# Linear attention into a Swish layer on one core: the first two batches' kv in quadrants, the numerators in rows of 64, and a new order of the start

## The chip, the core and the metric

The kernel runs on one core of a Trainium2 chip. A core has a matrix engine (PE, whose weight loads the profile lists as PEld), a vector engine (DVE), an activation engine (ACT), a general engine (POOL) and a queue engine (SP). The engines run on their own and wait for each other by semaphores; each takes its instructions in order. Results of PE land in PSUM, eight banks of 512 f32 values on each of 128 partitions; everything else lives in SBUF, and DMA queues move data to and from memory. The metric is the device time of one execution in microseconds (us). Before the change three runs took 277.32, 277.26 and 275.57 us, a median of 277.26.

## The reference

Inputs are q, k and v of 8 batches, 8 heads, 576 positions and 64 elements, and the weights `w_in` (512 x 2048), `w_out` (2048 x 512) and `beta` (2048).

```python
phi = lambda x: np.where(x > 0, x, np.exp(x) - 1.0) + 1.0
q_p, k_p = phi(q), phi(k)
kv  = einsum('bhsd,bhse->bhde', k_p, v)      # 64 x 64 for each head
z   = sum(k_p, axis=2)
num = einsum('bhsd,bhde->bhse', q_p, kv)
den = einsum('bhsd,bhd->bhs', q_p, z)[..., None] + 1e-6
x   = (num / den)                            # rows (b, s), columns (h, d): 4608 x 512
h   = x @ w_in
g   = h * sigmoid(beta * h)
out = g @ w_out                              # 4608 x 512, f32
```

## The kernel before

**Layout.** A batch's 576 positions are 64 groups of 9 (`G`, `J`). Heads are held in fours: `pr` (0 or 1) picks a block of four heads, a row half `a` of the 128 partitions and an index `il` within the half pick the head. `phi` is the minimum of an exponential on ACT (`phi_exp`, L162) and `max(x, 0) + 1` on DVE (`phi_relu`, L167; `phi_min`, L174). A batch's positions make four tiles of 128 rows (t = 0 to 3), which H and Y of the batch use, and a tile of 64 rows (t = 4), which goes to `xT_tail` and is worked off for all batches together at the end.

**A batch.** phi(k) and v give kv (and z, as a 65th column of ones in `vaug`, from batch 1 on). phi(q) is transposed, the numerators are a product of its transpose and kv, DVE divides by the denominators into `xs_sb`, and the result is transposed again into `xT`. H is 16 blocks `ff` of 128 columns, four matmuls each over 512 columns (`h_mm`, L401), followed by Silu on ACT (`silu`, L409), which writes `g`. Y of batch 0 is 16 quarters `y_mm(0, t, i)`: tile t, and four blocks of `w_out_sb[i]`, four matmuls each (L416). From batch 1 on, Y uses a scheme with fewer products (`y_fast`, L796).

**Order.** The program's order is written out by hand (`manual_schedule`): each engine takes its instructions in the order of the text, and only the semaphores are made by the framework. A PSUM tile gets one of the slots of its pool and has to wait until the last reader of the slot's tile before it is done; accesses of two engines to one bank of one tile are put in the order of the text. Before the change there are four single banks for the whole run (`bank`, pool `hps`), four more for the start (`bank1`, pool `fps`), and after `first.close()` (L630) two pairs of banks (`banks`, pool `wps`) in place of the latter.

**The start, batch 0 (L482 to L629).** q and k are loaded in halves on the SP queue, v in two halves (`v0b`) on the POOL queue, held back by a small copy `gate` that needs the first half of q. `idle(n)` issues n matmuls of 512 columns whose result nobody reads. After phi(q) and its transposes (`q_half`, `q_last`), DVE copies the first half of the transposes (`q_copy`, L505) ahead of `phi_min` of k's first half, and ACT copies the second (L544). PE then sums phi(k) over the positions (`z_sums`, L515) and forms kv with 128 columns for a pair of heads at once (`kv_first`, L526), of which half is not wanted: DVE masks it (`kv_mask`, L535). `zbd` (L553) spreads z to a masked matrix, twenty matmuls give the denominators `dps` (L563), `denom` (L570, L571) adds 1e-6 and inverts them, `numer_first` (L582, L586) gives the numerators in four matmuls over all 128 rows and divides, `x_first` transposes and copies, and `h_first(t)` does four blocks of H for 128 columns of tile t. The order on PE is z_sums(0), kv_first(0), z_sums(1), the denominators, kv_first(1), numerators of three tiles, and then transposes, H and the rest of the numerators by turns. Twelve blocks of H over 512 columns follow.

**Between H of batch 0 and H of batch 1 (L640 to L711).** Here `w_out` is scaled by 1/beta (`w_out_scale`, L450 and L452), phi of batch 1 is made, and Y of batch 0 is interleaved with kv of batch 1 (`kv_both`, L222), which is copied in two casts of 64 partitions into a block matrix `kv_bd` (L234), its numerators (`numer_mm`, L297; `numer_xs`, L308 to L310), their transposes (`x_trans`, L381) and phi of batch 2. From batch 2 on kv goes to `kv_q` with one cast (L230).

Of the kernel before, what the change touches and what calls it, by code (L numbers as in the profile page):

```python
# [16 lines left out]
def kernel(  # L17
# [29 lines left out]
    first = ExitStack()  # L47
    fps = first.enter_context(tc.tile_pool(name="fps", bufs=4, space=bass.MemoryType.PSUM))
# [4 lines left out]

    def bank1(name, shape=None, dt=F32):
        return fps.tile(shape or [P, 512], dt, tag="f", name=name)
# [62 lines left out]
    kv_bd = consts.tile([P, 2, 2, 2, EA], BF16)  # L118
    nc.gpsimd.memset(kv_bd, 0.0)
# [19 lines left out]
    kvmask = consts.tile([P, 2, 2, EA], BF16)  # L139
    nc.vector.memset(kvmask, 0.0)  # L140
    nc.vector.memset(kvmask[:D, :, 0, :], 1.0)
    nc.vector.memset(kvmask[D:P, :, 1, :], 1.0)
# [4 lines left out]

    warm_ps = bank("warm_ps")
# [24 lines left out]
    def phi_min(b, a, pr):  # L173
        nc.vector.tensor_tensor(  # L174
            st[b, a][:, pr].rearrange("p j (h d) -> p j h d", h=2),
            st[b, a, pr, "e"].rearrange("p h j d -> p j h d"),
            st[b, a, pr, "r"].rearrange("p h j d -> p j h d"),
            ALU.min,
        )
# [32 lines left out]
    def kv_both(b):  # L212

        t = banks("kvp")
        for pr in range(2):
            for j in range(J):
                for il in range(2):  # L220
                    for a in range(2):
                        nc.tensor.matmul(  # L222
                            t[half(il), a, pr * EA : (pr + 1) * EA],
                            st[b, "k"][half(a), pr, j, il * D : (il + 1) * D],
                            vaug[b % 2][half(a), pr, j, il, 0:EA],
                            start=(j == 0), stop=(j == J - 1), skip_group_check=True,
                        )
        tv = t[:, :, 0 : 2 * EA].rearrange("p a (r e) -> p a r e", r=2)
        if b > 1:
            nc.vector.tensor_copy(kv_q[b % 2], tv)  # L230
            return
        st[b, "kv"] = kv_bd.rearrange("p a r h e -> p a r (h e)")
        for il in range(2):
            nc.vector.tensor_copy(kv_bd[half(il), :, :, il], tv[half(il)])  # L234
# [42 lines left out]
    def q_stat(b, t, hh, pr, n):  # L277
        if (b, "qTd") in st:
            return st[b, "qTd"][:, hh, pr * J + 2 * t : pr * J + 2 * t + n // G, :].rearrange(
                "p j g -> p (j g)"  # L280
            )
        return st[b, "qT"][:, pr, t, hh, 0:n]

    def rows_of(t):
        return P if t < NT - 1 else G

    def xs_tile(b, t):
        st[b, "xs", t] = xs_sb.rearrange("p i n -> p (i n)")[:, t * DM : (t + 1) * DM]
        n = rows_of(t)
        return st[b, "xs", t][:n].rearrange("p (i a d) -> p a i d", a=2, d=D)  # L290

    def numer_mm(b, t):
        n = rows_of(t)
        nps = st[b, "nps", t] = banks("nps")
        for hh in range(2):
            for pr in range(2):
                nc.tensor.matmul(  # L297
                    nps[:n, hh, pr * 2 * EA : (pr + 1) * 2 * EA],
                    q_stat(b, t, hh, pr, n), st[b, "kv"][:, hh, pr, :],
                    start=True, stop=True, skip_group_check=True,  # L300
                )

    def numer_xs(b, t):
        n = rows_of(t)
        nv = st[b, "nps", t][:n, :, 0 : 4 * EA].rearrange("p a (h e) -> p a h e", h=4)
        den = work.tile([P, 2, 7], F32, tag="den", name="den")[:, :, 0:4]
        rden = work.tile([P, 2, 7], F32, tag="rden", name="rden")[:, :, 0:4]
        nc.vector.tensor_scalar(den[:n], nv[:, :, :, D], 1e-6, None, ALU.add)  # L308
        nc.vector.reciprocal(rden[:n], den[:n])
        nc.vector.tensor_mul(  # L310
            xs_tile(b, t), nv[:, :, :, 0:D], rden[:n, :, :, None].to_broadcast([n, 2, 4, D])
        )
# [58 lines left out]
    def x_dst(b, t):  # L371
        if t < NT - 1:
            return xT[b % 2][:, :, 2 * t : 2 * t + 2].rearrange("p i r n -> p r i n")
        return xT_tail[:, :, b].rearrange("p i r n -> p r i n")

    def x_trans(b, t, eng, tp=None):
        n = rows_of(t)
        if tp is None:
            tp = banks("xtp", [P, KC, P], BF16)
        for p in range(KC):  # L380
            nc.tensor.matmul(  # L381
                tp[:, p, :n], st[b, "xs", t][:n, p * P : (p + 1) * P], identity[:n, :n],
                is_transpose=True, start=True, stop=True, skip_group_check=True,
            )
        copy(eng, x_dst(b, t), tp[:, :, :n].rearrange("p (r i) n -> p r i n", i=2))

    def x_trans_dma(b, t=NT - 1):
        for pr in range(2):
            nc.sync.dma_start_transpose(
                out=xT_tail[:, :, b, pr],  # L390
                in_=st[b, "xs", t][: rows_of(t), pr * HM : (pr + 1) * HM],
            )
# [98 lines left out]
    qtp = [bank1("qtp", [P, 1024], BF16) for _ in range(2)]  # L491
    phi_part(0, "q", 0)
    q_half(0, 0, qtp[0])
    idle(3)
    phi_part(0, "q", 1)
    q_half(0, 1, qtp[1])
    t8 = bank1("qtp8", [P, 2 * P], BF16)
    q_last(0, t8)
    bps = bank("bps", [P, FC])
    nc.tensor.matmul(bps, beta_row, ident16, is_transpose=True, start=True, stop=True)  # L500
    idle(4)
    x = xin(0, "k", 0)
    phi_exp(0, "k", 0, x)
    phi_relu(0, "k", 0, x)
    q_copy(nc.vector, 0, 0, qtp[0])  # L505
    phi_min(0, "k", 0)


    zps = [bank("zps") for _ in range(2)]
# [10 lines left out]
    kvp0 = [bank1("kvp0") for _ in range(2)]  # L520
    kv0 = consts.tile([P, 2, 2, 2 * D], BF16)

    def kv_first(pr):
        for j in range(J):
            for hh in range(2):
                nc.tensor.matmul(  # L526
                    kvp0[hh][:, pr * P : (pr + 1) * P],
                    st[0, "k"][half(hh), pr, j, :],
                    v0b[half(hh), 2 * pr : 2 * pr + 2, j, :],
                    start=(j == 0), stop=(j == J - 1), skip_group_check=True,  # L530
                )

    def kv_mask(pr):
        for hh in range(2):
            nc.vector.tensor_mul(  # L535
                kv0[:, hh, pr].rearrange("p (h d) -> p h d", h=2),
                kvp0[hh][:, pr * P : (pr + 1) * P].rearrange("p (h d) -> p h d", h=2),
                kvmask[:, hh, :, 0:D],
            )

    z_sums(0)
    idle(1)
    phi_part(0, "k", 1)
    q_copy(nc.scalar, 0, 1, qtp[1])  # L544
# [3 lines left out]
    kv_first(0)  # L548
    z_sums(1)
    idle(1)  # L550
    kv_mask(0)
    for hh in range(2):
        nc.vector.tensor_mul(  # L553
            zbd[:, hh], zps[hh][:, 0:2, None].to_broadcast([P, 2, 2]), kvmask[:, :, :, 0]
        )
    dps = bank("dps", [P, NT, 2, 2, 2])
    den0 = consts.tile([P, NT, 8], F32)
    rden0 = consts.tile([P, NT, 8], F32)
    for t in range(NT):
        n = rows_of(t)  # L560
        for hh in range(2):
            for pr in range(2):
                nc.tensor.matmul(  # L563
                    dps[:n, t, hh, pr], st[0, "qT"][:, pr, t, hh, 0:n], zbd[:, hh, pr, :],
                    start=True, stop=True, skip_group_check=True,
                )
    dv = dps.rearrange("p t a b c -> p t (a b c)")
# [5 lines left out]
    kv_first(1)  # L573
    denom(P, slice(0, NT - 1))
    kv_mask(1)

    def numer_first(t):
        n = rows_of(t)
        nps = bank1("nps0", [P, 2, 2, P])
        for hh in range(2):  # L580
            for pr in range(2):
                nc.tensor.matmul(  # L582
                    nps[:n, hh, pr], st[0, "qT"][:, pr, t, hh, 0:n], kv0[:, hh, pr, :],
                    start=True, stop=True, skip_group_check=True,
                )
        nc.vector.tensor_mul(  # L586
            xs_tile(0, t),
            nps[:n].rearrange("p a b (c d) -> p a (b c) d", d=D),
            rden0[:n, t].rearrange("p (a i) -> p a i", a=2)[:, :, :, None].to_broadcast(
# [3 lines left out]

    def x_first(t, eng):
        x_trans(0, t, eng, bank1("xtp0", [P, KC, P], BF16))

# [3 lines left out]
    def h_first(t):  # L600
        if not hp0:
            hp0.extend(bank("h_ps") for _ in range(4))
        for ff in range(4):
            h_mm(xT[0], ff, hp0[ff], t * P, (t + 1) * P)

    for t in range(3):
        numer_first(t)
    denom(G, slice(NT - 1, NT))
    x_first(0, nc.scalar)
    numer_first(3)  # L610
    x_first(1, nc.scalar)
    h_first(0)
    numer_first(4)
    x_first(2, nc.scalar)
    h_first(1)
    x_first(3, nc.scalar)
# [3 lines left out]
    nc.vector.reciprocal(rbeta, beta_c)  # L620
    h_first(2)
    x_first(4, nc.vector)
    h_first(3)
    for ff in range(4):
        silu(0, ff, hp0[ff])
    for ff in range(4, 8):
        hp = bank1("h_ps")
        h_mm(xT[0], ff, hp)
        silu(0, ff, hp)  # L629
    first.close()  # L630
    wps = ctx.enter_context(tc.tile_pool(name="wps", bufs=2, space=bass.MemoryType.PSUM))
# [20 lines left out]
    phi_min(1, "q", 0)  # L652
    phi_min(1, "q", 1)
# [18 lines left out]
    w_out_scale(nc.scalar, 3)  # L672
    for t in range(2):
        y_mm(0, t, 2, yps[t])
    kv_both(1)
    phi_tile(2, "q")
    phi_tile(2, "k")
    y_mm(0, 2, 2, yps[2])
    numer(1, 0)
    y_mm(0, 3, 2, yps[3])  # L680
# [247 lines left out]
```

## Time and profile before

| | |
|---|---|
| profiled execution, device time | 276.86 us |
| its span, first to last instruction | 275.1 us |
| median of three runs | 277.26 us |
| PE busy | 267.2 us, 97% of the span |
| DVE, ACT, POOL busy | 168.2, 173.4, 44.3 us |
| granted TensorE clock, mean | 0.991 |
| PE busy from 0 to 17.80 us | 14.48 us |
| PE busy from 17.80 to 42.68 us | 24.78 of 24.88 us |
| PE busy from 42.68 to 51.92 us | 8.65 of 9.24 us |
| PE busy from 51.92 us on | 219.35 of 223.18 us |

Times in the views are counted from the first instruction. The timeline gives start and length in us, engine, line, operation and tile, the number of instructions merged into the row, and in brackets the idle time of the engine before it with what ended it. The chain of waits follows the execution back from its last instruction, at each step to what released it. A busy PE is not a PE at full speed: the column PEclk says what share of its clock was granted.

### The profile page before, as it was taken

Reading aid. Unit: us, or ns where it says so; the run is one execution under the profiler, and the core shown is the slowest. Engines: PE = TensorE matmul, PEld = TensorE weight load, DVE = VectorE, ACT = ScalarE, POOL = GpSimd, SP = SyncE. Lnnn points to the kernel's source line nnn. Section 1 sums busy time; section 2 is a strip of 40 time slices with the busy share of each in tenths; the row PEclk is TensorE's granted clock in tenths of the full one; section 3 lists DMA queues with packets and bytes.
Section 4 is the critical chain, followed back from the end, with each engine's and each line's share of the span. In section 5 each row is a group of like instructions: output and inputs, shape, how many; then the busy total and the mean of one; then the engine's idle time right before and its main releaser. Section 6 shows DMA issues by size and latency. Waiting matters only on the chain.

```text
span 275.1 us, 6478 instructions
## 1 busy us (share of the span) xinstructions
PE 267.2 (97%) x2756; PEld 173.2 (63%) x2761; DVE 168.2 (61%) x322; ACT 173.4 (63%) x237; POOL 44.3 (16%) x64
## 2 busy tenths in 40 slices
PE   7799999999999999999999999999999999999994
PEld 2585455445865487548754875488548845874693
DVE  4771775999896687566757685768463513342532
ACT  5728897976875785579457946794573077117600
POOL 5822102034003122131213112300000000000000
PEclk9979999999999999999999999999999999999998
DMA  7999999467978996996599659965530040032013
GB/s 255 237 206 351 262 382 256 150 110 225 219 112 170 287 176 115 283 212 65 103 281 211 78 99 279 223 75 88 153 75 13 21 133 0 2 71 82 2 38 114
DMA packets 48956, 42.76 MB, mean 155 GB/s; under 512 B 30352, under 2 KB 40736, under 8 KB 48928
## 3 DMA queue, kind: packets, MB, share of 16 engines
q0 software_dynamic: 13040, 23.40, 36.6%
q1 hardware_dynamic: 35568, 18.75, 32.1%
q8 instruction: 21, 0.34, 0.5%
q10 hardware_dynamic: 320, 0.20, 0.2%
q14 instruction: 7, 0.06, 0.1%
HBM read 36.71 MB, written 9.44 MB: 168 GB/s over the span
## 4 chain that ended last, share of the span: by engine, by line
PE 92%; DVE 3%; DMA 2%; issue 1%; SPq 0%; ACT 0%; DVEq 0%
PE h_ps L401 46%; PE yd L796 10%; PE ya L796 10%; PE yb L796 9%; PE yc L796 5%; PE y_ps L416 4%; DMA stage<-in_k_dram 2%; PE kvp L222 2%; PE nps L332 2%; PE yb L768 1%; PE xtp L381 1%; DVE r L167 1%; PE nps L582 1%; DVE phi_k L174 1%; PE nps L297 1%
## 5 line engine op out<-in xcount | busy, mean ns | idle before, releaser
L409 ACT ACTIVATE g<-h_ps,beta_c 128x512 bf16<-128x512 f32 x144 | 97.6, 687 | 62.0 <-PE h_ps L401 61.8
L401 PE MATMUL h_ps<-xT,w_in 128*128 128x512 bf16 (+1 forms) x560 | 114.5, 361 | 0.1
L401 PEld LDWEIGHTS <-w_in 128*128 128x128 bf16 x624 | 57.4, 98 | 62.1 <-issue 0.2
L796 PEld LDWEIGHTS <-stage 128*128 128x128 bf16 x480 | 46.9, 98 | 5.6 <-issue 0.2
L796 PEld LDWEIGHTS <-g 128*128 128x128 bf16 x384 | 37.5, 98 | 6.0
L796 PE MATMUL ya<-w_out,g 128*128 128x256 bf16 x256 | 30.6, 273 | 0.0
L723 DVE TENSOR_TENSOR stage<-g 128x1024 bf16<-128x1024 bf16 x16 | 12.6, 787 | 22.0 <-ACT g L409 22.0
L727 DVE TENSOR_TENSOR stage<-g 128x1024 bf16<-128x1024 bf16 x16 | 11.8, 739 | 21.8 <-ACT g L409 21.8
L240 POOL CAST vaug<-vf 128x1152 bf16<-128x1152 f32 x11 | 13.6, 1259 | 40.5 <-DMA vf<-in_v_dram 40.5
L347 DVE TENSOR_TENSOR xs_sb<-nps,rden 128x448 bf16<-128x448 f32 (+2 forms) x24 | 18.2, 758 | 0.8
L162 ACT ACTIVATE e<-xk 128x1152 bf16<-128x1152 bf16 (+1 forms) x15 | 16.7, 1160 | 2.2 <-DMA xk<-in_k_dram 2.2
L162 ACT ACTIVATE e<-xq 128x1152 bf16<-128x1152 bf16 x14 | 15.6, 1159 | 1.4 <-DMA xq<-in_q_dram 1.1
L820 DVE TENSOR_TENSOR u<-yc,r 128x512 f32<-128x512 f32 x8 | 5.5, 691 | 17.5 <-PE yc L796 16.6
L155 ACT ACT_TABLE_LOAD x12 | 15.4, 1283 | 0.2
L796 PE MATMUL yd<-ws,stage 128*128 128x256 bf16 x128 | 15.3, 273 | 0.0
L796 PE MATMUL yc<-ws,stage 128*128 128x256 bf16 x128 | 15.3, 273 | 0.0
L796 PE MATMUL yd<-ws,g 128*128 128x256 bf16 x128 | 15.3, 273 | 0.0
L416 PE MATMUL y_ps<-w_out,g 128*128 128x512 bf16 x60 | 14.6, 379 | 0.3 <-issue 0.2
L174 DVE TENSOR_TENSOR phi_q<-e,r 128x1152 bf16<-128x1152 bf16 x16 | 12.3, 766 | 3.7 <-ACT e L162 2.6
L401 PE MATMUL h_ps<-xT_tail,w_in 128*128 128x512 bf16 x64 | 14.0, 379 | 0.0
L367 POOL COPY xT_tail<-xT 128x256 bf16<-128x256 bf16 x6 | 3.1, 518 | 65.4 <-DMA xT<-xs_sb 65.4
L174 DVE TENSOR_TENSOR phi_k<-e,r 128x1152 bf16<-128x1152 bf16 x16 | 12.8, 803 | 1.4
(101 smaller groups left out, 256.5 us busy)
## 6 DMA issues: line engine op xcount, KB each, us to landing
vf<-in_v_dram POOLq DMA_DIRECT2D x7, 1152.0 KB, 9.2
out_dram<-y SPq DMA_DIRECT2D x29, 256.0 KB, 3.8
xq<-in_q_dram POOLq DMA_DIRECT2D x7, 576.0 KB, 12.2
xk<-in_k_dram POOLq DMA_DIRECT2D x7, 576.0 KB, 15.4
w_in<-in_moe_w_in_dram POOLq DMA_DIRECT2D x4, 512.0 KB, 12.7
g<-in_moe_w_out_dram POOLq DMA_DIRECT2D x2, 1024.0 KB, 18.1
stage<-in_moe_w_out_dram POOLq DMA_DIRECT2D x2, 1024.0 KB, 21.3
stage<-in_q_dram SPq DMA_DIRECT2D x2, 576.0 KB, 4.1
```

The costliest lines, as they stand in the source:

```text
L155: nc.scalar.activation(act0, warm[:, 0:1], func)
L162: nc.scalar.activation(e, x, ACTF.Exp)
L174: nc.vector.tensor_tensor(st[b, a][:, pr].rearrange("p j (h d) -> p j h d", h=2), st[b, a, pr, "e"].rearrange("p h j d -> p j h d"), st[b, ...
L222: nc.tensor.matmul(t[half(il), a, pr * EA : (pr + 1) * EA], st[b, "k"][half(a), pr, j, il * D : (il + 1) * D], vaug[b % 2][half(a), pr, j, ...
L240: eng.tensor_copy(dst, src)
L347: nc.vector.tensor_mul(xs_sb[:, ils, v0 * D : v1 * D].rearrange("p i (u d) -> p i u d", d=D), pv[:, :, :, 0:D], rden[:, :, :, None].to_bro ...
L401: nc.tensor.matmul(hp[:, c0:c1].rearrange("p (t n) -> p t n", n=n), w_in_sb[ff // 4][:, kc, (ff % 4) * P : (ff % 4 + 1) * P], xm, start=(k ...
L409: nc.scalar.activation(g_sb[b % 2][:, ff, :], hp, ACTF.Silu, scale=beta_c[:, ff : ff + 1])
L416: nc.tensor.matmul(yp[:, c0:c1], g_sb[b % 2][:, ff, t * P : (t + 1) * P], w_out_sb[i][:, c, c0:c1], start=(ff == 0), stop=(ff == FC - 1), ...
L723: nc.vector.tensor_sub(gs[2][:, c], g[:, c, 0:HM], g[:, c, HM:512])
L727: nc.vector.tensor_add(gs[0][:, c], g[:, c, HM:512], g[:, c2, HM:512])
L796: nc.tensor.matmul(ps[:, p * HM : (p + 1) * HM], lhs(c, p), rhs(c), start=(first and p == 0 and c == 0), stop=True, skip_group_check=True,)
```

## The change

The kv matrices of batches 0 and 1 are formed head by head in quadrants of PE (64 rows by 64 columns), so that nothing has to be masked; `kv_mask`, `kv_bd` and its memset on POOL go. The numerators of both batches are made with 64 rows of contraction, eight matmuls for a tile instead of four, the two row halves into two banks. The column order of `xs_sb` changes with that, and with it the copies into `xT`. PSUM is four single banks and two pairs from the start on. In the single banks sit `zps` (two), `t8b` (the last transposes of q, beta, and the denominators) and `warm_ps`; later one bank `xtp0` for all transposes of the start and three for the first blocks of H, so that `h_first` does three blocks instead of four and a thirteenth follows over 512 columns. On PE, kv_first(0) and half of kv_first(1) come ahead of z_sums(1), the other half ahead of the denominators, and the denominators are made tile 0 first. The first copy of q's transposes moves from DVE to ACT, ahead of phi(k); `phi_min` of k's second half is done in two halves. There are three more `idle` matmuls. In the stretch after H of batch 0, three quarters of Y stand ahead of `kv_both(1)` instead of two, one between it and the numerators, none between the first two numerators; the scaling of `w_out_sb[3]` is shared by ACT and POOL; and `phi_min` of q stands ahead of `phi_relu` of k.

```diff
-        st[b, "kv"] = kv_bd.rearrange("p a r h e -> p a r (h e)")
-        for il in range(2):
-            nc.vector.tensor_copy(kv_bd[half(il), :, :, il], tv[half(il)])
+        nc.vector.tensor_copy(
+            kv_q[b % 2], t[:, :, 0 : 2 * EA].rearrange("p a (r e) -> p a r e", r=2)
+        )
...
     def numer_mm(b, t):
-        n = rows_of(t)
+        n, e = rows_of(t), EA if b else D
         nps = st[b, "nps", t] = banks("nps")
-        for hh in range(2):
-            for pr in range(2):
-                nc.tensor.matmul(
-                    nps[:n, hh, pr * 2 * EA : (pr + 1) * 2 * EA],
-                    q_stat(b, t, hh, pr, n), st[b, "kv"][:, hh, pr, :],
+        for pr in range(2):
+            for a in range(2):
+                for il in range(2):
+                    c = 2 * pr + a
+                    nc.tensor.matmul(
+                        nps[:n, il, c * e : (c + 1) * e],
+                        st[b, "qT"][half(il), pr, t, a, 0:n],
+                        (kv_q[1] if b else kv0)[half(il), a, pr, :],
...
+    zps = [bank("zps") for _ in range(2)]
+    t8b = bank("t8b")
     warm_ps = bank("warm_ps")
...
     phi_part(0, "q", 1)
-    q_half(0, 1, qtp[1])
+    q_copy(nc.scalar, 0, 0, qtp[:, 0])
+    q_half(0, 1, qtp[:, 1])
...
-    q_copy(nc.vector, 0, 0, qtp[0])
-    phi_min(0, "k", 0)
+    phi_part(0, "k", 0)
...
+    kvp0 = banks("kvp0")
+    kv0 = consts.tile([P, 2, 2, D], BF16)
+
+    def kv_first(pr, ils=range(2)):
+        for il in ils:
+            for j in range(J):
+                for a in range(2):
+                    nc.tensor.matmul(
+                        kvp0[half(il), a, pr * D : (pr + 1) * D],
+                        st[0, "k"][half(a), pr, j, il * D : (il + 1) * D],
+                        v0b[half(a), 2 * pr + il, j, :],
...
     z_sums(0)
-    idle(1)
-    phi_part(0, "k", 1)
+    idle(2)
+    x = xin(0, "k", 1)
+    phi_exp(0, "k", 1, x)
+    phi_relu(0, "k", 1, x)
+    for il in range(2):
+        phi_min(0, "k", 1, slice(il, il + 1))
...
     kv_first(0)
+    kv_first(1, (0,))
     z_sums(1)
-    idle(1)
-    kv_mask(0)
+    kv_first(1, (1,))
     for hh in range(2):
         nc.vector.tensor_mul(
-            zbd[:, hh], zps[hh][:, 0:2, None].to_broadcast([P, 2, 2]), kvmask[:, :, :, 0]
+            zbd[:, hh], zps[hh][:, 0:2, None].to_broadcast([P, 2, 2]), ilmask
         )
+    nc.vector.tensor_copy(kv0, kvp0[:, :, 0:P].rearrange("p a (r d) -> p a r d", r=2))
...
+    def x_first(t, eng):
+        if not xtb:
+            xtb.append(bank("xtp0", [P, KC, P], BF16))
+        x_trans(0, t, eng, xtb[0])
...
+    def h_first(t, ffs=range(3)):
+        if not hp0:
+            hp0.extend(bank("h_ps") for _ in range(3))
+        for ff in ffs:
             h_mm(xT[0], ff, hp0[ff], t * P, (t + 1) * P)
...
+    d_sums(0)
+    denom(P, slice(0, 1))
+    idle(1)
+    numer_mm(0, 0)
+    xs_first(0)
+    for t in range(1, NT):
+        d_sums(t)
+    denom(P, slice(1, NT - 1))
+    numer_mm(0, 1)
+    xs_first(1)
+    x_first(0, nc.scalar)
+    numer_mm(0, 2)
+    xs_first(2)
     denom(G, slice(NT - 1, NT))
-    x_first(0, nc.scalar)
-    numer_first(3)
+    idle(2)
+    h_first(0, (0, 1))
     x_first(1, nc.scalar)
-    h_first(0)
-    numer_first(4)
+    h_first(0, (2,))
+    numer_mm(0, 3)
+    xs_first(3)
     x_first(2, nc.scalar)
     h_first(1)
-    x_first(3, nc.scalar)
+    numer_mm(0, 4)
+    xs_first(4)
...
+    x_first(3, nc.scalar)
     h_first(2)
     x_first(4, nc.vector)
     h_first(3)
-    for ff in range(4):
+    for ff in range(3):
         silu(0, ff, hp0[ff])
-    for ff in range(4, 8):
-        hp = bank1("h_ps")
+    for ff in range(3, 8):
+        hp = bank("h_ps")
...
-    w_out_scale(nc.scalar, 3)
-    for t in range(2):
+    for t in range(3):
         y_mm(0, t, 2, yps[t])
     kv_both(1)
+    for c in range(4):
+        w_out_scale((nc.scalar, nc.gpsimd)[c % 2], 3, (c,))
...
-    y_mm(0, 2, 2, yps[2])
+    y_mm(0, 3, 2, yps[3])
     numer(1, 0)
-    y_mm(0, 3, 2, yps[3])
     numer(1, 1)
```

## The prediction

> **What bounds the kernel now.** I read the page first: PE is busy for 97% of the span and has 92% of the chain that ended last. So only two things count: PE's idle or slow time, and work put on it or taken off it. A table of PE's busy time by stretch puts the slack in the first 17.8 us and in 42.68 to 51.92 (0.59 us idle), which are the stretches that the change touches; in between, PE misses 0.1 us. The chain of waits then says what sets the start:
>
> ```profile
> 11.63 0.77 DVE phi_k L174
> ...
> 12.45 0.38 PE zps L515 x18
> ...
> 13.15 0.70 PE dps L563 x20
> 13.85 1.08 PE kvp L526 x18
> 14.93 0.29 DVE kv L535
> ...
> 15.26 1.33 PE nps L582 x11
> 16.59 0.55 PE xtp L381 x4
> ...
> 17.17 0.59 ACT xT L238
> ...
> 17.80 1.05 PE h_ps L401 x16
> ```
>
> The reader sees a serial path from phi(k) to the first H at 17.80, with the second half of kv (13.85) behind the denominators. From 17.80 PE is full; H of batch 0 ends and Y's first record starts at 32.95. The clock, by slices of 1 us (PEclk is third from the end):
>
> ```profile
> 13.00:14.00 1.00, 1.00 (x27) 0.89 (x28) 0.20 (x3) 0.89 (x2) 0.69 (x1) 0.93 1.24 205
> 14.00:15.00 1.00, 1.00 (x19) 0.74 (x14) 0.52 (x3) 0.00 (x0) 0.05 (x1) 0.50 1.25 208
> ...
> 16.00:17.00 1.00, 1.00 (x11) 0.80 (x9) 1.00 (x3) 0.00 (x0) 0.72 (x1) 0.50 1.25 213
> 17.00:18.00 1.00, 0.91 (x14) 0.79 (x12) 0.97 (x5) 0.83 (x2) 0.03 (x1) 0.86 1.23 201
> ```
>
> 0.93 and 0.86 put half clock from 13.87 to 17.28, right on this path. Third, the second half of v (the transfer issued at 5.93, the view of its tile):
>
> ```profile
> L99 POOL DMA_DIRECT2D vf<-in_v_dram x1: 721/721/721, 5.9 to 5.9; - x1
> ...
> DMA to landing us min/median/max: 7.1/7.1/7.1
> ```
>
> It lands at 5.93 + 7.09 = 13.02. Nobody waits for it before: kv_first(1) comes at 13.78.
>
> **Part 1: to the first numerator.** Without the transposes' copy (0.67) on DVE, phi_min of k's first half starts when its exponential ends, at 9.76 instead of 10.12, and the two halves of the last phi_min (0.76 whole; 0.38 to 0.45 each) end at about 11.7 and 12.05 instead of 12.39. The copy on ACT (0.99) fits between its exponentials, 7.03 to 8.56; without that gap it would delay phi(k) by 0.99. POOL's memset of kv_bd (0.52 at 1.56) goes, but POOL then waits for q at 4.38 anyway: nothing.
>
> The 0.35 us is not kept. kv_first(1) now stands on PE ahead of z_sums(1) and needs v, so PE waits at 12.2 until 13.06, and behind that wait queue z_sums(1), the denominators and all else on PE; DVE and ACT wait for them. From there: half of kv_first(1), 18 matmuls. The nearest row is kv_both, 72 in 0.78, so (0.78 - 0.19)/71 = 0.0083 each with four quadrants by turns; here only two take turns, so I take twice that, 0.30 in all (ends: 0.15, and 0.50 from kv_first's row of 18 in 0.68 less one length). Then z_sums(1) at 13.45 (0.23 + 0.16 latency), zbd on DVE until 14.1, and the other half of kv_first(1), mostly at half clock, until 14.55. The copy of kv is one cast of 0.42 (L230's form) instead of masks: 15.01. The denominators of tile 0 (0.17 + 0.03 + 0.20) follow on DVE: 15.4. The eight matmuls of 64 rows start at 15.05 and end near 15.55; the first division starts at 15.58 (15.77 before). PE owes d_sums of tiles 1 to 4, a numerator and the transposes at half clock, the copy on ACT takes 0.59, and H starts at 17.84. **Part 1 sums to 0** (17.84 against 17.80), at full clock throughout to -0.95 (16.85).
>
> **Part 2: the first tiles of H.** Work moves: 4 x 4 matmuls of a tile become 12, and a thirteenth block over 512 columns (4 x 0.216 = 0.86) takes the fourth's place; equal, if PE is full. I don't think that it is. (a) The second of three banks is by the order of slots that of `t8b`, whose last reader is denom of tile 4, which stands on DVE behind the divisions of tiles 0, 1 and 2 (0.69 each, and 0.45 for denom of 1 to 3): about 18.25. PE, at 18.06 after the first block, waits 0.25 (0.5 at full clock, where it comes sooner); nothing, if another slot is second. (b) One bank holds all transposes: per tile transposes 0.39, ACT 0.59 and two semaphores make 1.05 us, against 0.67 + 0.22 + 0.2 of PE work, so waits of about 0.2 before tile 2 and 0.15 each before tiles 3 and 4. (c) The numerators of tiles 3 and 4 switch PE to 64 rows and back, 0.1 each way, and give back half of 4 x 0.056: 0.1 each. (d) The thirteenth block takes the bank that DVE's last copy empties, behind four small beta operations: 0.15. Together 0.25 + 0.5 + 0.2 + 0.15 = **+1.1**; from 0.3 without (a) and with half of the rest, to 1.5.
>
> The switch is shown here:
>
> ```profile
> 42.37 0.38 PE L416 MATMUL y_ps<-w_out,g 128*128 128x512 bf16 x1
> ...
> 42.68 0.78 PE L222 MATMUL kvp<-vaug,phi_k 64*64 64x65 bf16 x72
> ```
>
> The next matmul would have started at 42.37 + 0.216 = 42.59; in the new mode it starts 0.09 later. [...]
>
> **Part 3: around kv of batch 1.**
>
> ```profile
> 43.59 0.87 DVE L234 CAST kv_bd<-kvp 64x260 bf16<-64x260 f32 x2 [1.71 <-PE kvp L222]
> ...
> 44.52 0.41 PE L297 MATMUL nps<-kv_bd,qT 128*128 128x130 bf16 x4
> ...
> 45.40 0.69 DVE L310 TENSOR_TENSOR xs_sb<-nps,rden 128x512 bf16<-128x512 f32 x1
> ```
>
> Count from kv_both's last start, 43.27. Before: numerator 0 at +1.25 (it waits for the casts), transposes at +2.88, filled by a quarter of Y (0.86), H at 51.92, +8.65. After: the single cast ends at +0.75, but a quarter of Y lasts until +1.0, so 0.45 of DVE's gain stays behind it; numerator 0 at +1.09, then nothing for PE until DVE has done 0.17 + 0.20 + 0.69 with gaps, transposes at +2.62: PE idles over 1 us. From there the chain numerator, division, transposes runs as before: H at +8.2. As kv itself starts a quarter later (+0.865), H comes at +9.07: **+0.4** (from 0, if the later waits for buffers shrink too, to +0.65, the whole uncovered quarter less 0.2). phi_relu of k is 0.83 later on DVE: w_out_scale(2) ends near 40.6, its first use at 40.87, and phi_min of k at 42.0, kv at 43.5: hidden. POOL's two scalings are not in the trace: 512 values at POOL's cast (1259 ns for 1152) or copy (518 for 256) are 0.56 to 1.04 each; after the landing at 43.54 both are done by 45.7, needed from 48: hidden, and every us beyond that would be paid.
>
> **Sum.** 276.86 (the profiled execution, 1.8 around its span) + 0 + 1.1 + 0.4 = 278.3; I say **278.2**. The profiled one is 0.4 below the median of the three runs, so that the median after may be as much higher.
>
> **Rivals.** *The clock stays up* (0.25). For: two more dummies (0.43) ahead of kv_first. Against: kv_first keeps half of the array idle, and the wait for v is a new gap. Part 1 becomes -0.95, part 2 +1.35: 276.86 + 0.4 + 0.4 = 277.7.
>
> *Faster* (0.13). v comes 1 us sooner than in this one profile, say at 12.0, so that kv_first(1) follows without a wait, the clock stays up and the slots are free (a is 0): 277.7 - 1.0 - 0.5 = 276.2. For: one run of before, 275.57, is 1.3 below the profile, so the start can be shorter. Against: nothing in the change moves that transfer.
>
> *Slower: the clock is not released at 17.28* (0.20). [...]
>
> **The numbers.** The forecast, half clock as before, has 0.42. Leaving out the lower half of the fast case and the upper half of the slow one gives 275.8 to 279.6. A measurement of this kernel tells about 1% from no change, 274.5 and 280.0 on either side of 277.26: faster 0.04, slower 0.09, the same 0.87.
>
> **What would show it.** Part 1: PE's first kv_first(1) waits for a DMA near 13.0; the first H at 17.8, or 16.9 with PEclk at 1.00. Part 2: gaps on PE ahead of the second block of H and of the transposes of tiles 2 to 4; Y's first matmul at 34, not 33. Part 3: PE idle for 1 us between numerators and transposes of batch 1. From H of batch 1 on, everything should be shifted evenly: if later batches change, or if v lands early, I am wrong.

## The result and the profile after

The changed kernel takes **278.66 us** (median of 19 executions, 277.03 to 280.54), the kernel before beside it 276.33 us (275.46 to 277.32): a ratio of 1.0078, with a 95% interval of 1.0059 to 1.0096. The forecast was 278.2 in a range of 275.8 to 279.6, and the chance on "within 1%" was 0.87. Against the kernel before the forecast was a loss of 0.9 us (277.26 to 278.2), and 2.33 us were measured. That the number was close is partly luck, as the steps below show.

The profiled execution of after took 277.03 us with a span of 275.3. It is the shortest of the 19, and its clock is never halved in the start; most of the others differ in this, so the profile alone doesn't explain the median. First the chain of waits of the changed kernel (start, length, what):

```profile
5.92 6.76 DMA vf<-in_v_dram
...
12.73 0.47 PE kvp L510 x18
13.20 0.31 PE zps L498 x18
13.51 0.42 PE kvp L510 x18
13.95 0.44 DVE kv L536
14.43 0.29 PE nps L281 x8
14.72 0.60 PE t8b L545 x16
...
16.16 0.54 PE warm_ps L148 x2
16.70 0.52 PE h_ps L386 x8
17.22 0.24 PE xtp L366 x4
17.48 0.59 ACT xT L227
18.07 0.04 issue
18.11 0.38 PE xtp L366 x4
```

The chain now goes through the transfer of v, as the prediction's part 1 said: kv_first(1) waits for it (0.78 us on PE), and z_sums(1), the cast of kv and the denominators follow in a row. The first H starts at 16.61 instead of 17.80. Behind it there is something new: PE waits for ACT's copy of the transposes (17.48, 0.59) before it can do the next ones. The clock by slices of 1 us of the same kernel (share of the slice, then busy shares of PE, PEld, DVE, ACT, POOL, and PEclk third from the end):

```profile
13.00:14.00 1.00, 1.00 (x53) 0.90 (x46) 0.28 (x3) 0.79 (x2) 0.72 (x1) 1.00 1.25 208
14.00:15.00 1.00, 0.66 (x24) 0.64 (x22) 0.86 (x4) 0.00 (x0) 0.00 (x0) 1.00 1.24 204
...
16.00:17.00 1.00, 1.00 (x18) 0.64 (x15) 0.99 (x2) 0.56 (x1) 0.62 (x1) 1.00 1.23 199
```

PEclk is 1.00 where before had 0.50. The timeline around kv of batch 1 (start, length, engine, line, operation, tile, number; in brackets the idle time ahead of it):

```profile
43.12 0.78 PE L215 MATMUL kvp<-vaug,phi_k 64*64 64x65 bf16 x72
44.05 0.81 PE L401 MATMUL y_ps<-w_out,g 128*128 128x512 bf16 x3 [0.16 <-issue]
44.80 0.42 PE L281 MATMUL nps<-kv_q,qT 64*128 64x65 bf16 x16
46.32 0.40 PE L366 MATMUL xtp<-identity,xs_sb 128*128 128x128 bf16 x4 [1.11 <-DVE xs_sb L295]
...
51.90 1.47 PE L386 MATMUL h_ps<-xT,w_in 128*128 128x512 bf16 x6
```

PE idles for 1.11 us between the numerators and the first transposes. Before, a quarter of Y stood between the first two numerators:

```profile
44.77 1.02 PE L416 MATMUL y_ps<-w_out,g 128*128 128x512 bf16 x4
```

Four spans compare the profiled executions, with the difference of each:

| | before | after | |
|---|---|---|---|
| start to first H | 17.80 | 16.61 | -1.19 |
| first H to first Y | 15.15 | 15.91 | +0.76 |
| first Y to H of batch 1 | 18.97 | 19.38 | +0.41 |
| H of batch 1 to the end | 223.16 | 223.36 | +0.20 |

They sum to +0.18: at its best the changed kernel is level with a profiled execution of before that had its clock halved for 3.41 us. The question left is where the other 2 us between the medians come from.

### The profile page after: what moved, and what is told of

It reads as the page before. It is cut to its first block, busy times and chain, and to the rows that moved or that the text cites. A ratio compares the mean times of both kernels' runs of the same rounds, so it can differ in the third digit from the quotient of the medians.

```text
span 275.3 us, 6612 instructions
## 1 busy us (share of the span) xinstructions
PE 265.3 (96%) x2822; PEld 170.8 (62%) x2828; DVE 165.2 (60%) x320; ACT 173.2 (63%) x236; POOL 46.0 (17%) x65
## 4 chain that ended last, share of the span: by engine, by line
PE 92%; DMA 4%; ACT 1%; DVE 1%; POOL 1%; issue 1%
PE h_ps L386 46%; PE yd L783 10%; PE ya L783 10%; PE yb L783 9%; PE yc L783 5%; PE y_ps L401 4%; DMA vf<-in_v_dram 2%; PE kvp L215 2%; PE nps L317 2%; DMA stage<-in_q_dram 1%; PE yb L755 1%; PE xtp L366 1%; ACT e L158 1%; ACT xT L227 1%; PE nps L281 1%
## 5 line engine op out<-in xcount | busy, mean ns | idle before, releaser
L714 DVE TENSOR_TENSOR stage<-g 128x1024 bf16<-128x1024 bf16 x16 | 12.0, 748 | 22.5 <-ACT g L394 22.5
L710 DVE TENSOR_TENSOR stage<-g 128x1024 bf16<-128x1024 bf16 x16 | 11.0, 687 | 22.1 <-ACT g L394 22.1
L170 DVE TENSOR_TENSOR phi_k<-e,r 128x1152 bf16<-128x1152 bf16 (+1 forms) x17 | 12.8, 765 | 1.8 <-ACT e L158 0.4
```

What stands on the lines that cost most here:

```text
L170: nc.vector.tensor_tensor(st[b, a][:, pr].rearrange("p j (h d) -> p j h d", h=2)[:, :, hs], st[b, a, pr, "e"].rearrange("p h j d -> p j h ...
L710: nc.vector.tensor_sub(gs[2][:, c], g[:, c, 0:HM], g[:, c, HM:512])
L714: nc.vector.tensor_add(gs[0][:, c], g[:, c, HM:512], g[:, c2, HM:512])
```

## The experiments

The theory was that two independent things add up: the new order costs about 1 us with the clock up, and its waits on PE let the clock fall in some executions. Rivals: it is the clock alone; or it is the three banks of the first H, which make `h_first` wait.

An execution's mean granted clock tells which case it is: it is 0.997 to 1.000 in the traces without a stretch of half clock ahead of the last microseconds, 0.991 or 0.992 in those with one of 3.41 us, and 0.988 in the two with 6.83 us. The mean doesn't tell where the stretch lies. With bounds between these values (0.996 and more, 0.990 to 0.995, 0.989 or less) all executions fall in groups (median in us, and number), before in the three comparisons beside the experiments:

| | none | 3.41 us | 6.83 us |
|---|---|---|---|
| changed | 277.30 (5) | 278.44 (6) | 279.20 (8) |
| changed, again | 277.11 (4) | 278.19 (4) | 279.46 (4) |
| before, first | 276.25 (25) | 276.78 (6) | 278.12 (4) |
| before, second | 276.29 (9) | 276.52 (5) | 278.35 (3) |
| before, third | 276.01 (20) | 276.78 (2) | 278.45 (1) |

**The changed kernel again** (e7), unaltered, for a second trace.

> The changed kernel unaltered, beside the others on one chip. Theory C: again three groups by mean granted clock, near 277.3, 278.4 and 279.2, and fewer than half of the executions at full clock; the kernel before beside it mostly at full clock, near 276.2. If the groups were a matter of the chip or the hour, the shares would be alike for both kernels.

278.19 us (276.89 to 279.84), ratio 1.0055 (1.0027 to 1.0083). Its trace fell in the third group. The clock by slices:

```profile
15.00:16.00 1.00, 1.00 (x26) 0.88 (x26) 0.89 (x3) 0.00 (x0) 0.00 (x0) 0.58 1.21 209
16.00:17.00 1.00, 1.00 (x15) 0.68 (x14) 0.90 (x3) 0.38 (x1) 0.75 (x1) 0.50 1.28 207
...
21.00:22.00 1.00, 1.00 (x15) 0.75 (x13) 0.00 (x0) 0.07 (x1) 0.00 (x0) 0.50 1.25 257
22.00:23.00 1.00, 1.00 (x20) 0.90 (x16) 0.84 (x3) 0.55 (x1) 0.75 (x1) 1.00 1.10 367
```

Half clock runs from 15.17 to 21.99, twice 3.41. The first H comes at 17.67 (16.61 in the trace above) and the first Y at 35.19 (32.52): 2.67 us more. Of these, 0.29 are v's: here it lands later, and kv_first(1) starts at 13.02 instead of 12.73. The other 2.4 are the stretch of 6.83 us.

**Waits filled** (e1). Six more `idle` matmuls (dummies, below) stand where PE waits.

```diff
-    idle(4)
+    idle(6)
     phi_part(0, "k", 0)
...
     kv_first(0)
+    idle(3)
     kv_first(1, (0,))
...
-    idle(1)
+    idle(2)
     numer_mm(0, 0)
```

> The changed kernel with six more dummy matmuls of 512 columns where its profile shows PE waiting: two ahead of the first z_sums, three between kv_first(0) and the half of kv_first(1) that waits for v, one more ahead of the first numerator. Theory C (clock): the executions of the changed kernel fall into three groups by their mean granted clock, 0.998 to 1.000 near 277.5 us, 0.991 to 0.994 near 278.5 and 0.985 to 0.987 near 279.3, that is, none, one or two stretches of 3.41 us at half clock, and the median of 278.66 is mostly that. With the waits filled nearly all executions should have 0.998 or more and the median should be 277.0 to 277.6, about 1.2 below the changed kernel. Theory O (order): the loss lies in the order of the work, which the dummies don't change: 278.3 to 279.0, or more, since they stand in PE's way.

277.39 us (276.93 to 279.12), ratio 1.0038 (1.0014 to 1.0062), and all twelve executions kept the clock up (means of 0.998 to 1.000). The chain of waits of this run:

```profile
12.13 0.75 PE warm_ps L148 x3
12.88 0.02 issue
12.90 0.47 PE kvp L510 x18
13.37 0.31 PE zps L498 x18
13.68 0.40 PE kvp L510 x18
```

The dummies end as v lands (12.86), and in this trace they cost nothing: the first H is 3.94 us behind the landing, 3.92 without them. So half clock is worth 278.66 - 277.39 = 1.3 us of the changed kernel's median, or 0.8 by its second measurement (278.19), and 277.39 is within 0.3 of the executions that had none of it (277.30, 277.11). What remains of the ratio, 0.4%, is the order's.

**The same in before** (e4), as a control: three more dummies ahead of k's phi and one between kv_first(0) and z_sums(1).

```diff
-    idle(4)
+    idle(7)
     x = xin(0, "k", 0)
...
     kv_first(0)
+    idle(1)
     z_sums(1)
```

> The kernel before with four more dummy matmuls in its waits: three ahead of the first z_sums (7 instead of 4) and one between kv_first(0) and z_sums(1). Theory C: the kernel before loses one stretch of half clock (13.87 to 17.28 in its profile) in most executions; without it its first H comes 0.7 to 0.9 earlier: 275.4 to 275.7 against 276.3, and a mean clock of 0.998 or more. If the stretch costs nothing, because DVE and DMA hold the start: 276.3.

276.46 us (275.94 to 277.34), ratio 0.9997 (0.998 to 1.0013); all twelve with the clock up (0.997 to 1.000). The forecast of 275.4 to 275.7 missed: it took the profile's stretch of half clock for the usual case, and most executions of the kernel before (54 of the 75 in the table) have no such stretch by their mean clock, so that it has almost nothing to win here. Its trace gives what the first stretches take at full clock: first H at 17.15, first Y at 32.30, H of batch 1 at 51.28. Against it the filled version of the changed kernel stands at 16.80, 32.71 and 52.09: 0.35 ahead, 0.41 behind, 0.81 behind. One trace fixes such a difference only roughly: with the same order of the start and the clock up, the first H of e9 and e11 (below) comes at 17.59 and 17.76.

**Y's quarters back** (e2). Two quarters ahead of kv_both(1), one between the first two numerators; all else as in the changed kernel.

```diff
-    for t in range(3):
+    for t in range(2):
         y_mm(0, t, 2, yps[t])
     kv_both(1)
...
-    y_mm(0, 3, 2, yps[3])
+    y_mm(0, 2, 2, yps[2])
     numer(1, 0)
+    y_mm(0, 3, 2, yps[3])
     numer(1, 1)
```

> The changed kernel with the quarters of batch 0's Y around kv of batch 1 as before: two ahead of it, one between it and the first numerators, one between the first two numerators. By part 3 of the prediction the new place of the quarters costs 0.4 us, so that this should be 0.4 below the changed kernel, 278.2 to 278.3, with H of batch 1 starting 8.6 to 8.7 after the last start of kv instead of 8.6 plus 0.87 of a quarter ahead. Rival: the stretch is held by ACT and by the landing of w_out's last quarter and batch 2's q, so that moving the quarters makes no difference (within 0.1). Theory C adds that the spread of 2 us and the three groups stay.

277.83 us, ratio 1.0037 (1.0011 to 1.0062). By groups it is 276.83, 277.67 and 278.47, or 0.47, 0.77 and 0.73 below the changed kernel's (0.28, 0.52 and 0.99 below its second measurement). The forecast was 0.4. In the trace, first Y to H of batch 1 takes 18.52 instead of 19.38:

```profile
46.57 0.30 PE L281 MATMUL nps<-kv_q,qT 64*128 64x65 bf16 x8
46.80 1.04 PE L401 MATMUL y_ps<-w_out,g 128*128 128x512 bf16 x4
47.77 0.30 PE L281 MATMUL nps<-kv_q,qT 64*128 64x65 bf16 x8
48.10 0.40 PE L366 MATMUL xtp<-identity,xs_sb 128*128 128x128 bf16 x4
```

The quarter (1.04) covers the division, and the wait of 1.11 is gone. The new place of the quarters costs 0.86, one whole quarter; the single cast and the rows of 64 give 18.97 - 18.52 = 0.45 back.

**z_sums(1) ahead of the wait for v** (e3).

```diff
     kv_first(0)
-    kv_first(1, (0,))
     z_sums(1)
-    kv_first(1, (1,))
+    kv_first(1)
```

> The changed kernel with z_sums(1) ahead of all of kv_first(1), so that z doesn't queue behind the wait for v. By part 1 of the prediction kv is then ready earlier by z_sums(1) and two switches of PE's mode, 0.31 + 0.1, and the first division and H of tile 0 follow 0.3 to 0.4 earlier: 278.3. Rival: the first division is held by the denominators on DVE, not by kv: no difference. [...]

278.02 us, ratio 1.0043 (1.0017 to 1.007); by groups 276.94, 278.06 and 279.16, that is 0.36, 0.38 and 0.04 lower (0.17, 0.13 and 0.30 against the second measurement). PE's timeline of this run:

```profile
12.09 0.38 PE L498 MATMUL zps<-ones,phi_k 64*128 64x1 bf16 x18
12.74 0.66 PE L510 MATMUL kvp<-vf,phi_k 64*64 64x64 bf16 x36 [0.28 <-DMA vf<-in_v_dram]
13.34 0.25 PE L544 MATMUL t8b<-zbd,qT 128*128 128x2 bf16 x4
```

The sums of z fit into the wait, and the first division starts 1.58 us behind v's landing instead of 2.10. It doesn't save the clock: here half clock runs from 15.71 to 19.12.

**Four banks for the first H**, first alone (e5) and then with e2, e3 and five dummies (e6). The transposes then share the two pairs of banks with the numerators, and the numerators of tile 2 go behind the first H.

```diff
-    def h_first(t, ffs=range(3)):
+    def h_first(t, ffs=range(4)):
...
-            hp0.extend(bank("h_ps") for _ in range(3))
+            hp0.extend(bank("h_ps") for _ in range(4))
...
-        x_trans(0, t, eng, xtb[0])
+        x_trans(0, t, eng)
...
-    for ff in range(3, 8):
-        hp = bank("h_ps")
+    pair = banks("h_ps")
+    for ff in range(4, 8):
+        hp = pair[:, ff - 4] if ff < 6 else bank("h_ps")
```

> The changed kernel with four single banks for the first blocks of H again: the transposes of the start go through the pairs of banks, denom of tile 4 and the third numerator move by one place to fit, blocks 4 and 5 of H take a pair. By part 2 of the prediction three banks cost PE 0.5 to 1 us between the first H and the first Y (15.9 us in the changed kernel's profile, 15.15 in that of before); with four this should be 15.2 to 15.4, and the time at full clock 276.6 to 276.8 instead of 277.3. Rival: the 0.76 us are the numerators in rows of 64 and their switches of mode, which stay: 15.8 and no difference. Theory C (clock): the share of executions with half clock stays.

> All at once: four banks, z_sums(1) ahead of kv_first(1), the quarters of Y as before, and five dummies in the waits. If the terms found so far add up (at full clock 277.3 less 0.5 to 0.8 for the quarters, 0.36 for z, 0.5 to 0.7 for the banks) and the clock stays up, the median is 275.4 to 275.9, below the kernel before (276.56 in the last comparison, 276.25 at full clock). If the terms hide each other or transfers become the bound: 276.2 or more.

280.76 us, ratio 1.0161 (1.0122 to 1.02), and 278.5 us, ratio 1.0068 (1.0044 to 1.0093). Both miss, in part by a wait that the edit itself made. From PE's timeline of the second:

```profile
24.63 0.59 PE L386 MATMUL h_ps<-xT,w_in 128*128 128x512 bf16 x2 [1.55 <-ACT g L394]
```

Blocks 4 and 5 are two banks of one tile, and the Silu of block 4, written ahead of block 5's matmuls, has to be done first. Without these 1.55 us the second would stand near 276.95, still 1 us above its forecast. So the banks were tried once more (e8), with both blocks' matmuls ahead of both Silus, and the six dummies of e1:

```diff
+    pair = banks("h_ps")
+    for ff in range(4, 6):
+        h_mm(xT[0], ff, pair[:, ff - 4])
+    for ff in range(4, 6):
+        silu(0, ff, pair[:, ff - 4])
```

> e5_four_banks once more, with blocks 4 and 5 of H issued both ahead of their Silu: in e5_four_banks the matmuls of block 5 stood behind the Silu of block 4, since both are in one tile, 1.6 us of PE's time that had nothing to do with the question; and with the dummies of e1_fill to hold the clock, so that it is to be compared with e1_fill (277.39). If three banks cost PE the time (prediction, part 2): 276.7 to 276.9, and 15.2 to 15.4 us from the first H to the first Y. If the numerators' switches of mode and the work that now stands behind the first division cost it: 277.3 to 277.6, and 15.8 to 16.0 us.

278.83 us, ratio 1.0094 (1.006 to 1.0128), above both forecasts. First H to first Y takes 16.02 us, as much as with three banks (15.91), with a single wait of PE in it (0.24, for ACT's copy, ahead of the first H itself). One more numerator stands in it now, and the waits that the fourth bank saves go to that. So four banks, as tried, bring nothing back, and the rival falls as far as this version goes; four banks with the numerator in its old place were not tried. It doesn't explain the time, though: in the traces H of batch 1 starts 0.15 later than in e1's, and the way from there to the end takes 0.93 more (224.36 against 223.43). Why was not found.

**Three parts undone** (e10): Y's quarters as in e2, z_sums(1) as in e3, and five dummies.

```diff
-    idle(4)
+    idle(6)
     phi_part(0, "k", 0)
...
     kv_first(0)
-    kv_first(1, (0,))
     z_sums(1)
-    kv_first(1, (1,))
+    idle(2)
+    kv_first(1)
...
-    idle(1)
+    idle(2)
     numer_mm(0, 0)
```

> The changed kernel with dummies in its waits, the old order of Y's quarters, and z_sums(1) ahead of kv_first(1): the three costs found so far undone together. If they add up (277.39 with dummies, less 0.5 to 0.75 and 0.36): 276.2 to 276.5, level with the kernel before. If a transfer (v, or the last quarter of w_out) becomes the bound: 276.8 or more.

276.59 us (276.09 to 278.56), ratio 1.0013 (0.9993 to 1.0034): level with before, and between the two forecasts. Terms from above give 277.39 - 0.86 - 0.36 = 276.2. H of batch 1 starts at 50.97, 0.95 earlier than in before's profile, and in this trace the lead is lost again at 78 us. The timeline of DVE in this run:

```profile
75.35 0.46 DVE L163 TENSOR_SCALAR r<-xq 128x1152 bf16<-128x1152 bf16 x1
76.67 0.76 DVE L170 TENSOR_TENSOR phi_q<-e,r 128x1152 bf16<-128x1152 bf16 x1 [0.85 <-ACT e L158]
77.34 0.68 DVE L818 TENSOR_TENSOR y<-yb,u 128x512 f32<-128x512 f32 x1
```

and of PE:

```profile
75.39 1.91 PE L784 MATMUL yd<-ws,g 128*128 128x256 bf16 x16
78.08 1.91 PE L784 MATMUL yb<-w_out,stage 128*128 128x256 bf16 x16 [0.78 <-DVE y L818]
```

PE is at 75.39 with work that before does at 76.19, but batch 3's q, issued at 63.9 and 11.4 us under way, lands at 75.33 (73.42 in before's trace). Its exponential starts at 75.41, and DVE's phi(q), written ahead of the addition `y`, waits for that. PE starts `yb` at 78.08, and before does at 78.09.

**One part alone in before**: the single cast and rows of 64 for batch 1, with Y's quarters as they were (e9); and the same with the new places of the quarters (e11). Both carry the dummies of the control.

```diff
-        for il in range(2):
-            nc.vector.tensor_copy(kv_bd[half(il), :, :, il], tv[half(il)])
+        nc.vector.tensor_copy(kv_q[b % 2], tv)
...
-        for hh in range(2):
-            for pr in range(2):
...
-                    q_stat(b, t, hh, pr, n), st[b, "kv"][:, hh, pr, :],
...
+        for pr in range(2):
+            for a in range(2):
+                for il in range(2):
...
+                        st[b, "qT"][half(il), pr, t, a, 0:n],
+                        kv_q[1][half(il), a, pr, :],
```

> The kernel before, with its old start and its old order of Y's quarters, and of the change only batch 1's kv copied by one cast and its numerators in rows of 64; four dummies in the waits of the start keep the clock up. The traces so far put the way from the first Y to H of batch 1 at 18.97 us in the kernel before and 18.52 where the changed kernel has the old order of the quarters: this part alone should gain 0.45, 276.0 against 276.46 of the kernel before with the same dummies, and beat both kernels. Rival: the numerators in rows of 64, with their switches of mode, cost what the cast gains: 276.4 to 276.6.

> The kernel of e9_before_b1 with the quarters of Y in the changed kernel's order: three ahead of kv, one between kv and the first numerator, none between the first two. If the place of the quarters by itself costs a whole quarter (0.86 us, of which the single cast gave 0.45 back in the changed kernel): 276.8 to 276.9, 0.8 to 0.9 above e9_before_b1, and 19.4 us from the first Y to H of batch 1. Rival: 0.4, the net of the prediction's part 3, is the price of the place alone: 276.4.

First Y to H of batch 1 takes 18.52 and 19.37: the 0.45 and the 0.85 are the same as above, in another kernel. The times aren't, and both are above all their forecasts: 279.05 us, ratio 1.0084 (1.0059 to 1.0109), and 280.52, ratio 1.0128 (1.0087 to 1.0169). The waits of PE in the first of them, 53 to 160 us (line, what was waited for, us, times, longest):

```profile
PE h_ps L402 <- issue: 3.4, 1, 3.4
PE nps L330 <- DMA qTd<-phi_q: 1.1, 1, 1.1
PE yd L798 <- DVE u L823: 0.3, 1, 0.3
PE yb L798 <- DVE y L832: 0.2, 1, 0.2
```

Before has none of these in its profile. That one of 1.1 is batch 3's numerators, which in before start at 86.09, 0.53 behind the landing of q's transposes (85.56); here that landing is at 87.04, 6.4 us after its issue instead of 4.8. The 3.4 us at 144.4, ahead of H, has no releaser in the trace, and half clock begins within it (146.96 to 150.38). This profiled execution is one of two of the twelve near 283 us, so the 3.4 belongs to few of them; but also the other ten lie at 278.6.

The profiled execution of e11 is a usual one, 279.88 us with the clock up, and shows both waits again: 1.04 for the same transposes (6.4 us again) and 0.90 ahead of the same H. They are 1.94 of the 2.67 us by which its way from H of batch 1 to the end (225.83) is longer than in before's profile. Why these transposes take longer in both kernels was not found.

## Why the prediction was right, and where it was not

**Part 1 (0 with half clock, -0.95 without).** The mechanism held. The wait for v is there, 0.78 us, and z_sums(1) behind it costs what e3 gives back: 0.52 us on the way from v's landing to the first division, 0.17 to 0.36 in the medians with the clock up. The first H stands at 16.61 with full clock (16.85 forecast) and at 17.67 in the trace with half clock (17.84). The steps fit less well than the end: there the first division starts at 15.08 (15.58 forecast), since half clock begins only at 15.17. What failed is the frame. The sum started from 276.86 us, an execution with half clock from 13.87 to 17.28, and took that for the kernel before. Of its 75 executions beside the experiments 54 had no such stretch, so a part 1 that sums to 0 against that profile is a loss against the median. With the clock up on both sides, 16.80 and 16.61 stand against 17.15 in e4's trace, a gain of 0.35 to 0.54 where 0.95 was forecast.

**Part 2 (+1.1).** +0.76 was measured, within the bounds of 0.3 to 1.5, from other terms. (a) The slot of `t8b` comes third, not second, and delays the third block's matmuls by 0.14, not 0.25 to 0.5. (b) The shared bank of transposes costs two waits of 0.16, not 0.5. (c) The switch was right: in PE's timeline twelve H matmuls start at 18.33, 0.056 apart, and take 0.67, to 19.00, and the numerators start at 19.10. (d) cost nothing. The gap ahead of the second block and Y's first matmul at 34 were not seen (32.52 in the first trace, 35.19 in the second). A term was missing: PE fills the wait for the first division with the denominators of tiles 1 to 4 (0.60), and in exchange one numerator and one set of transposes that before does ahead of its first H come behind it. By the starts in PE's timeline, numerators, transposes and switches behind the first H take 1.56 us after (two numerators, four sets of transposes) and 1.21 before (one and three). With the three waits that is 0.35 + 0.46 = 0.81, against 0.76 measured. This account was read from the two traces; no run moved that work back by itself. The rows for the switch:

```profile
18.33 0.83 PE L386 MATMUL h_ps<-xT,w_in 128*128 128x128 bf16 x12
19.10 0.31 PE L281 MATMUL nps<-kv,qT 64*64 64x64 bf16 x8
```

So the switch from 128*128 to 64*64 cost 0.10 here, half of the 0.19 that one of kv's matmuls takes (median 192 ns in before's trace, the 0.19 in part 1's 0.0083).

**Part 3 (+0.4).** Right in each number: from kv's last start, 43.70, numerator 0 at +1.10 (1.09 forecast), transposes at +2.62 (2.62), H at +8.20 (8.2); in all +0.41. POOL's two scalings, not in the trace of before, took 0.69 each (bounds 0.56 to 1.04) and were hidden.

**Sum.** At full clock the order costs 277.30 - 276.25 = 1.05 us (276.25 is from the executions beside e1 to e4) or, in the second comparison, 277.11 - 276.29 = 0.82; the two filled kernels, e1 and e4, measured side by side, are 0.93 apart. The rest is the clock: 1.28 of the 2.33 us, and 0.70 of the 1.52 (278.19 - 276.67) of the second comparison.

**The rivals.** *The clock stays up* was priced at 277.7 and happened in 9 of 31 executions, at 277.3 and 277.1. *The clock is not released* had a price of 279.1, at most 280, on which the upper end of the range rests: an estimate of the author's, one more stretch of 3.41 us at half clock because PE would be too little busy, and no run shows what brings the clock back. What the runs showed in its place are executions with 6.83 us of half clock by their mean (15.17 to 21.99 in e7's trace): 12 of 31, at 279.2 and 279.5. The forecast, one stretch at 278.2, is the remaining 10, at 278.4 and 278.2. So the three cases were all true, one execution at a time, and the median falls on the middle one. The working treated them as alternatives with one outcome. *Faster* (276.2) didn't happen: v landed at 12.69 in the profile, 0.33 earlier than in before's, and PE still waited. "Everything shifted evenly from H of batch 1 on" holds for the changed kernel (+0.20). It doesn't hold for others: in their traces the way from H of batch 1 to the end takes 224.29 in e4, 224.36 in e8, 224.39 in e10 and 225.83 in e11, where before's takes 223.16.

No version here beats the kernel before.

## What to carry to other kernels

Where the clock can fall in a stretch, as here in 22 of 31 executions, one profile shows one case. Compare the mean clock over many executions, before and after, before a sum is made against a profile. Work that is moved ahead of a wait for another engine has to leave enough on the matrix engine to cover that wait: one quarter of Y in the wrong place cost all of its 0.86 us. And a lead won early can be lost at a later transfer that doesn't move with it, as in e10's trace (PE 0.80 us ahead of before at 75.39, 0.01 at 78.08).

## What was not expected of the hardware

**The clock and the busy share.** In the start, half clock began at 13.87 (before), 14.70 (e2), 15.17 (e7), 15.29 (e5) or 15.71 (e3), or not at all, and lasted 3.41 or 6.83 us. The times between the changes of the clock that the traces record are 6.83, 3.41 and 256.00 us in before, that is 2, 1 and 75 times 3.413, and 269.65 in the changed kernel's first trace, 79 times that. PE's busy share of the stretch ahead doesn't tell whether the clock falls or comes back. From the table by stretches, first of before, whose clock fell at 13.87 and came back at 17.28:

```profile
10.46:13.87 3.41, 2.48 (x79) 2.13 (x82) 2.48 (x7) 3.38 (x6) 2.69 (x4) 1.00 1.22 201
13.87:17.28 3.41, 3.25 (x38) 2.69 (x38) 2.54 (x7) 0.15 (x2) 0.94 (x2) 0.50 1.24 208
```

then of the changed kernel's second trace, whose clock fell at 15.17 and came back only at 21.99:

```profile
11.76:15.17 3.41, 2.54 (x112) 2.06 (x106) 1.02 (x6) 1.70 (x4) 1.57 (x3) 1.00 1.24 206
15.17:18.58 3.41, 3.41 (x44) 2.45 (x42) 2.61 (x7) 0.58 (x1) 0.75 (x1) 0.50 1.24 207
```

and of its first, whose clock stayed up (the stretch begins twice 3.413 us behind 4.23, where this trace's record of full clock begins):

```profile
11.06:14.47 3.41, 2.30 (x98) 1.87 (x100) 1.55 (x7) 2.71 (x5) 2.56 (x4) 1.00 1.24 206
```

The clock stayed up behind 2.30 us of 3.41 in one execution, and fell behind 2.54 in another (2.99 in e5's); it came back behind 3.25 in before, and didn't behind 3.41 in the changed kernel. So the busy share alone, on which the author's estimate for the slower rival rested, is not shown to decide it, though the price was right. Whether the quadrants, which use 64*64 of PE's 128*128, matter here is open; no run tests it. The 1.3 us of 277 that half clock is worth in the changed kernel are more than its order's single edits gave in the median (0.83 in e2, 0.64 in e3).

**Waits for issue.** e9 and e11 have gaps of 3.4 and 0.9 us on PE near 145 us that no semaphore or transfer of data ends. Both stand ahead of the same instruction of PE, and both end shortly behind a transfer of 16 KB on a DMA queue that the profile lists as "instruction": it ends at 146.49 and PE goes on at 147.77 in e9, 144.25 and 145.70 in e11. Two smaller gaps of the kind, 0.78 us in e5 and 0.15 in e8, end 1.40 and 1.28 us behind such a transfer. That PE waited for its instructions is the author's estimate from this; no run tests it, nor why they were late.
